# Pacing the FFN matmuls between the counting steps of a balanced router, its third token list in one go, and idle matmuls ahead of the first transposes

## The chip, the cores and the metric

One core of one Trainium2 chip. The metric is device microseconds of one execution, the median of several runs. A profile is one execution, so its span differs a little from the median. Several chips were used; each experiment is compared with runs of the kernel before on the same chip. Where two experiments ran on different chips, only their ratios to that kernel are compared, and what chips differ by is in no interval.

Words used below. An idle matmul is one whose result nobody reads. Half clock, or cold, means a granted clock of TensorE of 0.50; the cold stretches behind 200 us last 3.4 us or two to four times that, and one such unit is called a window.

## The reference, cut to what matters

An attention block makes `x` (3072 tokens of 384). A router then gives each of 8 experts exactly 384 tokens, in the order of the scores, and each expert runs its FFN on its tokens.

```python
logits = x @ w_gate
order = np.argsort(-logits.flatten())
for idx in order:                       # greedy, with a capacity of N // E per expert
    tok, e = idx // E, idx % E
    if assigned[tok] >= 0 or counts[e] >= cap: continue
    assigned[tok] = e; counts[e] += 1
for e in range(E):
    h = np.maximum(x[assigned == e] @ w1[e], 0.0)
    out[assigned == e] = h @ w2[e]
```

## The kernel before

The attention part (to about 165 us) is not touched. The router runs in seven rounds and a rest. A round makes `choices`, searches a threshold in two searches of four steps, assigns tokens, and closes one expert, whose token list is then built, so that the rows of `x` can be gathered and its FFN can run. The FFN is a queue of 51 pieces (3 transposes, 24 up, 24 down); TensorE runs pieces of it between the steps. A step finds one digit of the threshold, and ends with a matmul that hands this digit to VectorE. An assignment begins with matmuls into `sums`; a list ends with matmuls into `tokens`, behind which three gathers (DMAs that fetch 128 rows of `x` each) are issued. The order on TensorE and VectorE is the order of the program.

```python
def counts_beside(r, above, choice, slots):
    ...                                   # 3 matmuls, L501: lhsT = above, rhs = choice
    some(dve_work, 1)
    tt(own, ...); reduce(part, ...)       # VectorE
    some(pe_work, slots)
    nc.tensor.matmul(out=cnt, lhsT=pick_th, rhs=part, ...)               # L513

def search(choice, over, slots):
    for shift, slots in zip((12, 8, 4, 0), slots):
        tt(above, over, steps[shift], ALU.is_ge)                         # VectorE
        if slots:
            some(pe_work, slots[0])
            cnt = counts_beside(r, above, choice, slots[1])
        else:
            cnt = counts_alone(r, above, choice)
        some(dve_work, 1)
        tt(fills, ...); reduce(filled, ...)                              # VectorE
        if slots:
            some(pe_work, slots[2])
        nc.tensor.matmul(out=digit, lhsT=units[shift], rhs=filled, ...)  # L535
        some(dve_work, 1)
        tt(new, over, digit, ALU.add)                                    # VectorE
        over = new
    return over

# expert_list(): [members, place, index, lines] + six times in_line + [used, tokens]
#   place:  a matmul (L600);  index: starts the DMA of the expert's weights
#   tokens: 24 small matmuls (L653), three gathers by GpSimd, pe_work.extend(ffn(L))
# ffn(L):   [turn(0..2)] + [up(ft, d)] * 24 + [down(i, ft)] * 24

def idle_turns(n):
    for _ in range(n):
        nc.tensor.matmul(out=bank("idle", "H")[:, 0:CAP], lhsT=ones[:],
                         rhs=idle[:, 0:CAP], start=True, stop=True)
...
slots = (2, 1, 1)
for rnd in range(E - 1):
    ...                                   # choices, keys: VectorE
    over = search(choice, high, [slots if rnd else None] * 4)
    stt(over[:], over[:], 65536.0, low[:], ALU.mult, ALU.add)
    over = search(choice, over, [slots if rnd else None] * 4)
    some(dve_work, len(dve_work))
    assign(choice, over, (1, 8))          # starts with the matmuls into sums (L549)
    dve_work.extend(expert_list())
    if rnd == 0:
        while dve_work:
            some(dve_work, 1)
            idle_turns(3)
        idle_turns(12)
        ...
    if rnd == 1:                          # "in one go": the list is built at once
        while dve_work:
            some(dve_work, 1)
            some(pe_work, 1)
    close()                               # otherwise it is built in the next round's steps
```

Of the kernel before, what the change touches and what calls it, by code (L numbers as in the profile page):

```python
# [23 lines left out]
def kernel(  # L24
# [29 lines left out]
    nc = tc.nc  # L54

    B, H, S, DH = q.shape
# [10 lines left out]
    CAP = N // E  # L67
    TE = CAP // 128
# [14 lines left out]
    def const(shape, dtype, name):  # L83
        return consts.tile(shape, dtype, name=name, tag=name)
# [223 lines left out]
    ones = const([128, 128], BF16, "ones")  # L308
# [49 lines left out]
    idle = const([128, CAP], BF16, "idle")  # L358
# [5 lines left out]
    def col(t, *shape):  # L364

        return t.rearrange("p (c o) -> p c o", o=1).to_broadcast((128, NT) + shape)

    def row(t, n):

        return t.rearrange("p (o n) -> p o n", o=1).to_broadcast((128, NT, n))  # L370
# [5 lines left out]
    def rt(shape, name, dtype=FP32, bufs=2):  # L376
        return route.tile([128] + shape, dtype, name=name, tag=name, bufs=bufs)
# [4 lines left out]
    def tt(out_, a, b, op):  # L382
        nc.vector.tensor_tensor(out=out_, in0=a, in1=b, op=op)  # L383
# [8 lines left out]
    def reduce(out_, in_, op):  # L392
        nc.vector.tensor_reduce(out=out_, in_=in_, axis=AX_X, op=op)
# [11 lines left out]
    def high_keys(best, key, half, high):  # L405

        bits = best.bitcast(I32)
        ts(key, bits, 31, ALU.arith_shift_right, -2147483648, ALU.bitwise_or)
        tt(key, bits, key, ALU.bitwise_xor)
        ts(half, key, 16, ALU.logical_shift_right)  # L410
        nc.vector.tensor_copy(out=high, in_=half)
# [40 lines left out]
    def assign_and_run(begun, also=None, again=None):  # L452
# [5 lines left out]
        def bank(name, tag):  # L458
            return psum.tile([128, 512], FP32, name=name, tag=tag, bufs=BUFS[tag])
# [5 lines left out]
        pe_work, dve_work = deque(), deque()  # L465

        def some(queue, n):
            for _ in range(min(n, len(queue))):
                queue.popleft()()

        def choices():

            masked = rt([NT, E], "masked")
            tt(masked[:], logits[:], row(penalty[:], E), ALU.add)
            best = rt([NT], "best")
            reduce(best[:], masked[:], ALU.max)
            tt(masked[:], masked[:], col(best[:], E), ALU.is_equal)
            tt(masked[:], masked[:], row(first[:], E), ALU.mult)
            pick = rt([NT], "pick")
            reduce(pick[:], masked[:], ALU.max)  # L480

            taken = rt([NT], "taken")
            reduce(taken[:], assigned[:], ALU.max)
            stt(pick[:], taken[:], 100.0, pick[:], ALU.mult, ALU.add)
            choice = rt([NT, E], "choice", BF16)
            tt(choice[:], masked[:], col(pick[:], E), ALU.is_equal)
            return choice, best

        def counts_alone(r, above, choice):

            cnt = r[0:NTH, 0:E]
            for c in range(NT):
                nc.tensor.matmul(out=cnt, lhsT=above[:, c, :], rhs=choice[:, c, :],
                                 start=(c == 0), stop=(c == NT - 1))
            return cnt

        def counts_beside(r, above, choice, slots):

            m, n = NTH * CG, E * CG
            for c in range(0, NT, CG):  # L500
                nc.tensor.matmul(out=r[0:m, 0:n],  # L501
                                 lhsT=above[:, c:c + CG].rearrange("p c n -> p (c n)"),
                                 rhs=choice[:, c:c + CG].rearrange("p c e -> p (c e)"),
                                 start=(c == 0), stop=(c == NT - CG))
            some(dve_work, 1)
            own = rt([CG, E], "own")
            tt(own[0:m], r[0:m, 0:n].rearrange("p (g e) -> p g e", e=E), mine8[0:m], ALU.mult)
            part = rt([E], "part", FP16)
            with nc.allow_low_precision("a single count"):
                reduce(part[0:m, :], own[0:m].rearrange("p g e -> p e g"), ALU.max)  # L510
            some(pe_work, slots)
            cnt = r[0:NTH, n:n + E]
            nc.tensor.matmul(out=cnt, lhsT=pick_th[0:m, :], rhs=part[0:m, :], start=True, stop=True)  # L513
            return cnt

        def search(choice, over, slots):

            for shift, slots in zip((12, 8, 4, 0), slots):
                above = rt([NT, NTH], "above", BF16)
                tt(above[:], col(over[:], NTH), row(steps[shift][:], NTH), ALU.is_ge)  # L520
                r = bank("cnt", "r")
# [6 lines that stand above are left out]
                fills = rt([E], "fills")  # L528
                tt(fills[0:NTH, :], cnt, wanted[0:NTH, :], ALU.is_ge)
                filled = rt([1], "filled", BF16)  # L530
                reduce(filled[0:NTH, :], fills[0:NTH, :], ALU.max)
                if slots:
                    some(pe_work, slots[2])
                digit = r[:, 128:129]
                nc.tensor.matmul(out=digit, lhsT=units[shift][0:NTH, :],  # L535
                                 rhs=filled[0:NTH, :], start=True, stop=True)
                some(dve_work, 1)
                new = rt([NT], "over")
                tt(new[:], over[:], digit.to_broadcast((128, NT)), ALU.add)
                over = new  # L540
            return over
# [182 lines left out]
                   mybir.EngineType.Pool}  # L724
        def idle_turns(n):

            for _ in range(n):
                nc.tensor.matmul(out=bank("idle", "H")[:, 0:CAP], lhsT=ones[:],  # L728
                                 rhs=idle[:, 0:CAP], start=True, stop=True)

        with tc.manual_schedule(engines=engines):
            if begun is None:
                begun, part = begin()
                part(0, NCH)
            slots = (2, 1, 1)
            for rnd in range(E - 1):
                if rnd == 0:
                    choice, key, high = begun
                else:
                    choice, best = choices()  # L740
                    key, half, high = rt([NT], "key", I32), rt([NT], "half", I32), rt([NT], "high")
                    high_keys(best[:], key[:], half[:], high[:])
                low = rt([NT], "low")
                low_keys(key[:], low[:])
                over = search(choice, high, [slots if rnd else None] * 4)

                stt(over[:], over[:], 65536.0, low[:], ALU.mult, ALU.add)
                over = search(choice, over, [slots if rnd else None] * 4)
                some(dve_work, len(dve_work))
                assign(choice, over, (1, 8))  # L750
                dve_work.extend(expert_list())
                if rnd == 0:
                    while dve_work:
                        some(dve_work, 1)
                        idle_turns(3)
                    idle_turns(12)
                    if also:
                        dve_work.append(lambda: also(bank("hits", "r")))
                if rnd == 1:
                    while dve_work:  # L760
                        some(dve_work, 1)
                        some(pe_work, 1)
                close()
# [5 lines that stand above are left out]
            choice, _ = choices()  # L769
            tt(assigned[:], assigned[:], choice[:], ALU.add)  # L770
            nc.vector.memset(full[:], 1.0)
            some(pe_work, 4)
# [4 lines that stand above are left out]
            if again is not None:  # L777
                again.append(nc.values_load(beyond[0:1, 0:1], min_val=0, max_val=128))
            some(pe_work, len(pe_work))
# [18 lines left out]

    again = []
    assign_and_run(begun, in_range, again)  # L800


# [61 lines left out]
    with tc.If(again[0] > 0):  # L864
# [7 lines left out]
        with tc.For_i(0, B, 1) as b:  # L872
            x = pool.tile([128, NCH, D], FP32, name="xb", tag="xb", bufs=1)
            with tc.For_i(0, HP, 1) as hp:
                scan_pair(pool, x, b, hp)
            nc.sync.dma_start(
                out=xd[:, :].rearrange("(b c t) d -> b t c d", b=B, c=NCH)[
                    bass.ds(b, 1)].rearrange("b t c d -> (b t) c d"),
# [35 lines left out]
```

## Time and profile before

| | before |
|---|---|
| median, range of 4 runs | 568.57 us, 568.34 to 569.75 |
| span of the profiled run | 566.8 us |
| mean granted clock of TensorE | 0.938 |
| TensorE busy | 495.4 us, 87% |

The prediction shows the main lines. One view more, the waits (who waited, for what: us in total, times, longest), has the two waits that this case is about:

```profile
PE Xe L686 <- DMA xe<-xd,token: 13.8, 9, 4.9
...
PE cnt L501 <- DVE above L383: 3.5, 5, 1.1
```

The first is TensorE with an empty queue, waiting for gathered rows. The second is a count waiting for VectorE.

### The profile page before, as it was taken

The numbers are of one execution on the slowest core, as the hardware profiler recorded it, in microseconds if no ns is written. First come the engines' busy times: TensorE is split into PE (matmuls) and PEld (weight loads), VectorE is DVE, ScalarE is ACT, GpSimd is POOL, SyncE is SP. The second block draws the span as 40 slices with busy tenths as digits, with TensorE's granted clock in tenths as the row PEclk, the third lists the DMA queues.
The fourth block names the chain that finished last, engine by engine and source line by source line (L and its number), as shares of the span: only waits on it lengthen the run. The fifth ranks groups of instructions, "written<-read, shape, count | busy, mean of one in ns | idle before, by whom it ended". The sixth has DMA issues, their size and how long they took to land.

```text
span 566.8 us, 12225 instructions
## 1 busy us (share of the span) xinstructions
PE 495.4 (87%) x5031; PEld 310.8 (55%) x5031; DVE 290.5 (51%) x990; ACT 128.2 (23%) x301; POOL 114.2 (20%) x172
## 2 busy tenths in 40 slices
PE   3999999999974669969995798989989989999993
PEld 2688788888863334444542444545445556555551
DVE  6666566566754744572477267477585682000000
ACT  3455455543410011101200110111021021120310
POOL 3243333422300020050012101302212142101001
PEclk9999999999985579996999698999999999999998
DMA  8888998751010340070006106206134187100000
GB/s 176 178 184 173 206 194 173 166 126 50 32 45 1 114 151 0 1 279 26 1 14 250 43 0 235 73 1 236 56 127 153 37 279 258 42 0 29 14 15 31
DMA packets 118352, 59.08 MB, mean 104 GB/s; under 512 B 101648, under 2 KB 112912, under 8 KB 118288
## 3 DMA queue, kind: packets, MB, share of 16 engines
q1 hardware_dynamic: 111760, 44.06, 29.4%
q0 software_dynamic: 3072, 9.44, 5.1%
q10 hardware_dynamic: 3456, 4.72, 2.3%
q8 instruction: 41, 0.67, 0.5%
q14 instruction: 23, 0.19, 0.1%
HBM read 48.77 MB, written 9.44 MB: 103 GB/s over the span
## 4 chain that ended last, share of the span: by engine, by line
PE 61%; issue 18%; DVE 13%; POOL 4%; DMA 2%; ACT 1%; POOLq 0%; DVEq 0%; ACTq 0%
PE H L697 15%; PE O L708 13%; PE Y L239 4%; PE T L185 4%; PE A L222 3%; PE L L153 3%; PE Y L249 2%; PE L L157 2%; PE X L265 2%; PE dS L204 2%; DMA xe<-xd,token 2%; POOL out_dram L713 2%; PE idle L728 2%; POOL xe L663 1%; PE X L279 1%
## 5 line engine op out<-in xcount | busy, mean ns | idle before, releaser
L697 PE MATMUL H<-xeT,w 128*128 128x384 f32 x384 | 151.4, 526 | 4.9 <-ACT xeT L689 4.9
L708 PE MATMUL O<-w,hT 128*128 128x384 f32 x384 | 141.5, 506 | 0.0
L697 PEld LDWEIGHTS H<-xeT,w 128*128 128x128 f32 x384 | 69.1, 197 | 40.2 <-ACT xeT L689 6.4
L708 PEld LDWEIGHTS O<-w,hT 128*128 128x128 f32 x384 | 68.7, 192 | 37.0 <-issue 2.8
L713 POOL DMA_INDIRECT out_dram<-o,token x24 | 25.4, 1058 | 192.6 <-ACT o L712 192.0
L701 ACT ACTIVATE hT<-H 128x384 f32<-128x384 f32 x64 | 31.4, 491 | 135.9 <-PE H L697 134.4
L227 DVE COPY_PREDICATED am<-mask,A 128x512 f32<-128x512 int32 x48 | 32.4, 728 | 31.3 <-PE A L222 31.3
L712 ACT COPY o<-O 128x384 f32<-128x384 f32 x24 | 11.5, 479 | 141.7 <-PE O L708 141.7
L663 POOL DMA_INDIRECT xe<-xd,token x24 | 24.0, 1002 | 47.1 <-DVE over L383 26.0
L383 DVE TENSOR_TENSOR in_line<-line,count 128x512 bf16<-128x512 f32 x48 | 32.0, 699 | 0.1
L177 POOL TENSOR_TENSOR kg<-k,ek 128x384 f32<-128x384 f32 x24 | 25.5, 1065 | 27.2 <-ACT ek L165 21.4
L383 DVE TENSOR_TENSOR own<-cnt,mine 120x64 f32<-120x64 f32 x48 | 10.7, 222 | 38.9 <-PE cnt L501 38.7
L153 PE MATMUL L<-g,wcum 128*128 128x384 f32 x48 | 22.5, 551 | 7.9 <-DVE count L322 7.9
L501 PEld LDWEIGHTS <-above 128*120 128x120 bf16 x144 | 15.7, 142 | 22.1 <-DVE above L383 9.6
L239 PE MATMUL Y<-v,am 128*64 128x48 f32 x768 | 27.7, 224 | 0.0
L383 DVE TENSOR_TENSOR above<-over,steps 128x360 bf16<-128x360 f32 x49 | 26.1, 533 | 1.7
L239 PEld LDWEIGHTS Y<-v,am 128*64 128x64 f32 x768 | 24.5, 138 | 4.1 <-issue 3.7
L222 PE MATMUL A<-qT,kT 48*64 48x128 f32 x768 | 25.8, 272 | 0.0
L686 PE MATMUL Xe<-ident,xe 128*128 128x128 f32 x72 | 13.5, 324 | 13.8 <-DMA xe<-xd,token 13.8
L689 ACT COPY xeT<-Xe 128x384 f32<-128x384 f32 x24 | 10.8, 488 | 62.5 <-PE Xe L686 62.3
L162 DVE TENSOR_SCALAR dl<-L 128x384 f32<-128x384 f32 x24 | 13.4, 557 | 19.4 <-PE L L157 19.4
L629 POOL TENSOR_TENSOR past<-b,ramp_nt 128x48 f32<-128x48 f32 x8 | 2.4, 305 | 101.1 <-DVE b L383 83.6
(164 smaller groups left out, 633.4 us busy)
## 6 DMA issues: line engine op xcount, KB each, us to landing
w<-in_moe_w_dram SPq DMA_DIRECT2D x16, 1536.0 KB, 6.9
f<-in_f_logit_dram SPq DMA_DIRECT2D x24, 192.0 KB, 3.8
q<-in_q_dram SPq DMA_DIRECT2D x24, 192.0 KB, 3.9
k<-in_k_dram SPq DMA_DIRECT2D x24, 192.0 KB, 4.1
v<-in_v_dram SPq DMA_DIRECT2D x24, 192.0 KB, 4.0
xd<-x ACTq DMA_DIRECT2D x24, 192.0 KB, 3.4
xe<-xd,token POOLq DMA_INDIRECT x24
out_dram<-o,token POOLq DMA_INDIRECT x24
```

The costliest lines, as they stand in the source:

```text
L153: nc.tensor.matmul(out=Lv, lhsT=wcum[:], rhs=g[:, :, 0:DH], start=True, stop=True)
L177: nc.gpsimd.tensor_tensor(out=kg[:, :, 0:DH], in0=G["k"][:], in1=ek[:], op=ALU.mult)
L185: nc.tensor.transpose(out=T[:, 128 * hp:128 * hp + 128], in_=t[:, 2 * hp:2 * hp + 2, :].rearrange("t h d -> t (h d)"), identity=ident[:])
L222: nc.tensor.matmul(out=A[par][HC * j:HC * j + HC, 128 * hp:128 * hp + 128], lhsT=G["kT"][rows, hp, HC * j:HC * j + HC], rhs=G["qT"][rows, ...
L227: nc.vector.copy_predicated(am[:, par], mask[:].unsqueeze(1).to_broadcast((128, HP, 128)), A[par][:].rearrange("s (a t) -> s a t", t=128))
L239: nc.tensor.matmul(out=Y[par][HC * j:HC * j + HC, DH * hp:DH * hp + DH], lhsT=G["am"][:, par, hp, HC * j:HC * j + HC], rhs=G["v"][:, 2 * h ...
L383: nc.vector.tensor_tensor(out=out_, in0=a, in1=b, op=op)
L663: nc.gpsimd.indirect_dma_start(out=xe[:], out_offset=None, in_=xd[:, :], in_offset=bass.IndirectOffsetOnAxis(ap=token[:, i:i + 1], axis=0))
L697: nc.tensor.matmul(out=L["H"][:, 0:CAP], lhsT=L["w1"][:, d, 128 * ft:128 * ft + 128], rhs=xT[:, d, :], start=(d == 0), stop=(d == DC - 1))
L701: nc.scalar.activation(out=hT[:, ft, :], in_=L["H"][:, 0:CAP], func=AF.Relu)
L708: nc.tensor.matmul(out=L["O"][:, 0:D], lhsT=hT[:, ft, 128 * i:128 * i + 128], rhs=L["w2"][:, ft, :], start=(ft == 0), stop=(ft == FC - 1))
L713: nc.gpsimd.indirect_dma_start(out=outs[next(tiles)][:, :], out_offset=bass.IndirectOffsetOnAxis(ap=L["token"][:, i:i + 1], axis=0), in_=o ...
```

## The change

The intent: spend fewer pieces between the steps of rounds two and three, so that some are left when the next gather is under way; build the third list at once, as the second is; and keep TensorE from idling ahead of the first transposes. (The idle matmuls also write one tile of another pool now.)

```diff
         def idle_turns(n):
+            nothing = bank("nothing", "O")
             for _ in range(n):
-                nc.tensor.matmul(out=bank("idle", "H")[:, 0:CAP], lhsT=ones[:],
-                                 rhs=idle[:, 0:CAP], start=True, stop=True)
+                nc.tensor.matmul(out=nothing[:, 0:CAP], lhsT=ones[:], rhs=idle[:], start=True,
+                                 stop=True)
...
-            slots = (2, 1, 1)
+            pace = {0: None, 1: (1, 1, 1), 2: (1, 1, 1)}
...
-                over = search(choice, high, [slots if rnd else None] * 4)
+                slots = [pace.get(rnd, (2, 1, 1))] * 4
+                over = search(choice, high, slots)
...
-                over = search(choice, over, [slots if rnd else None] * 4)
+                over = search(choice, over, slots)
...
-                    idle_turns(12)
+                    idle_turns(27)
+                    for _ in range(TE - 1):
+                        some(pe_work, 1)
+                        idle_turns(4)
...
-                if rnd == 1:
+                if rnd in (1, 2):
```

## The prediction

> **What bounds the kernel now.** I read first the page of the run: the slices of busy tenths and clock, and the chain that ended last.
>
> ```profile
> PE   3999999999974669969995798989989989999993
> PEclk9999999999985579996999698999999999999998
> ...
> PE 61%; issue 18%; DVE 13%; POOL 4%; DMA 2%; ACT 1%; POOLq 0%; DVEq 0%; ACTq 0%
> ```
>
> A slice is 14.2 us. TensorE is full in the attention part (to about 165 us) and again from about 320 us on. Between lie dips in both rows. The first (slices 12 and 13) is the counting of the first round, which has no FFN work beside it yet; the change leaves it alone. The dips near 205, 255 and 310 us are what it aims at. Busy time by stretches of 10 us sizes two of them (columns: length, PE, PEld, DVE, ACT, POOL busy with counts, granted clock, DMA share, GB/s):
>
> ```profile
> 250.00:260.00 10.00, 4.20 (x34) 2.95 (x31) 4.84 (x21) 1.89 (x4) 3.94 (x4) 0.73 0.62 213
> 310.00:320.00 10.00, 5.27 (x23) 3.14 (x20) 2.16 (x11) 1.44 (x3) 2.90 (x3) 0.50 0.22 62
> ```
>
> Then the timeline of TensorE, at these three places (start, duration, line, tile, count, idle time before it and who ended it). The first is from a stretch at 184 us, the other two from one at 235 us:
>
> ```profile
> 199.44 2.60 PE L728 MATMUL idle<-idle,ones 128*128 128x384 bf16 x15
> 204.40 0.52 PE L686 MATMUL Xe<-ident,xe 128*128 128x128 f32 x3 [2.36 <-DMA xe<-xd,token]
> ...
> 207.40 0.87 PE L686 MATMUL Xe<-ident,xe 128*128 128x128 f32 x3 [0.77 <-DMA xe<-xd,token]
> ```
> ```profile
> 249.77 0.75 PE L653 MATMUL tokens<-number,in_line 128*128 128x6 bf16 x24
> 255.38 0.90 PE L686 MATMUL Xe<-ident,xe 128*128 128x128 f32 x3 [4.87 <-DMA xe<-xd,token]
> ...
> 303.41 0.91 PE L708 MATMUL O<-w,hT 128*128 128x384 f32 x2
> ...
> 309.33 0.81 PE L653 MATMUL tokens<-number,in_line 128*128 128x6 bf16 x24
> 313.90 0.90 PE L686 MATMUL Xe<-ident,xe 128*128 128x128 f32 x3 [3.76 <-DMA xe<-xd,token]
> ```
>
> Each expert's FFN is a queue of 51 pieces: 3 transposes, 24 up, 24 down. A piece (two instructions) costs 15.75/24 = 0.656 us where nothing interrupts. The queue runs dry twice: from 250.5 to 255.4 the second expert's gather is awaited, and from 304.3 to 313.9 hardly anything but counting runs, because the third list is built within the steps. The first idle time, 202.0 to 204.4, awaits the first gather.
>
> Last, what a step of the search costs when fed:
>
> ```profile
> 267.01 0.17 PE L535 MATMUL cnt<-filled,unit 15*128 15x1 bf16 x1
> 267.12 1.56 PE L697 MATMUL H<-xeT,w 128*128 128x384 f32 x4
> 268.51 0.30 PE L501 MATMUL cnt<-choice,above 128*120 128x64 bf16 x3
> 268.65 0.89 PE L697 MATMUL H<-xeT,w 128*128 128x384 f32 x2
> 269.47 0.17 PE L513 MATMUL cnt<-part,pick_th 120*15 120x8 f16 x1
> 269.57 0.91 PE L697 MATMUL H<-xeT,w 128*128 128x384 f32 x2
> 270.42 0.17 PE L535 MATMUL cnt<-filled,unit 15*128 15x1 bf16 x1
> ```
>
> 3.41 us from digit to digit: legs of 1.50 (two pieces), 0.96 and 0.95 (one each). Four pieces are 2.62 us, so 0.79 us is lost per step.
>
> **What the Trainium skill says.** "TensorE: Matmul & The Clock Gate", Part 1: activity is judged in free-running windows of 3413 ns, and a quiet one drops the clock to 4/8. The trace agrees: the granted clock is 0.50 in stretches, read in half microseconds, of about 206.7 to 213.5, 254.5 to 264.7, 309.1 to 322.7 and 343.2 to 346.6 us, that is 2, 3, 4 and 1 windows, on one grid. The same page, Part 4, says transposes do not count as busy in the same way; here the window ending at 206.7, with six of nine transposes in it, did go cold. "DMA: Bandwidth & Descriptors", "Anatomy of one DMA": about 2 us of fixed cost per transfer; that agrees: a gather's issue on GpSimd runs from 310.81 for 0.99 us, and TensorE can use the rows at 313.90, 2.1 us after that.
>
> From the trace I take a rule of thumb: counting each matmul's streaming time, the windows that went cold were up to about 0.35 full (that ending at 343.2 had 0.34), those with 0.39 to 0.46 stayed. This is an estimate.
>
> **The change part by part**, with S1, S2, S3 for the start of the assignment (first matmul into sums) of rounds two to four, which lies at 236.61, 288.28 and 332.14 us before. I counted the queue through both programs: pieces left there are 19, 18 and 35 before, 25, 31 and 29 after.
>
> (a) Idle matmuls. 15 took 2.60 us, so 30 (27 and the 3 of the list) end at 199.44 + 4.9 = 204.3, when the first gather lands: no gap. Four more (0.65 us each time) fit in the waits for the second and third gather (205.85, 207.40). The three landings do not move. But the clock stays high, so the half-clock stretch to 213.5 goes. Third transpose at 207.4, first up piece at 208.5, first digit of round two at 210.15 (210.42 before, with one piece fewer done after).
>
> (b) Steps of three pieces in rounds two and three. The leg with two pieces gets one. It is then bound by VectorE: over starts 0.21 us after the digit, above ends at 267.97, 0.96 after it, so the leg is about 1.03 and the step 0.96 + 0.95 + 1.03 = 2.94. A step loses 2.94 - 1.97 = 0.97, that is 0.18 us more than before; 16 steps cost 2.9 us. S1 is 210.15 + 7 x 2.94 + 0.2 (one more VectorE operation between the searches) + 0.84 = 231.8.
>
> (c) The second list. From sums to tokens took 13.16 us (236.61 to 249.77) with 19 pieces; one more makes 13.8, tokens at 245.6. Now five pieces are left, so the gather no longer is awaited. **But another wait takes its place**: the next count needs choices, keys and above from VectorE, and in round two that took from 198.83 (tokens) to 204.36 (end of above), 5.55 us. Only two pieces cover it: tokens 0.61 + 1.31 = 1.9, idle 3.65 us. Count at 251.2. By the rule of thumb a gap of this size goes cold with a chance of 0.95, for about 3.5 us in which steps lose some 0.43 of the time (a leg of 0.95 us takes 1.69 at half clock, 260.85 to 262.54): 1.5 us. S2 = 251.2 + 7 x 2.94 + 1.91 + 0.2 + 1.5 + 0.84, less 0.3 for the shorter transposes = 275.9.
>
> (d) Third list in one go. Again 13.8, tokens at 289.7, with 11 pieces left; three cover the wait, idle 3.0 us, count at 295.3; cold with 0.7, so 1.1 us. Round four keeps steps of four: S3 = 295.3 + 7 x 3.41 + 1.91 + 1.1 + 0.84 = 323.0. The hole of 304 to 314 us and the half clock to 322.7 go.
>
> Sum at S3: 332.14 - 323.0 = 9.1 earlier, with 6 pieces fewer left (3.9 us): **13.0 us gained**.
>
> (e) Given back in round five. The fourth list comes in the steps, as before, but only 4 pieces are left at its tokens (10 before). Four pieces and the counts last 4.04 us; the gather comes at 4.6, 5.8 and 7.1 us after tokens (as 309.33 to 313.90, 315.12, 316.46). That stalls 2.1 us, and the thin stretch goes cold with about 0.65: 1.0 more. Later lists have 14 and more pieces left.
>
> (f) The start of a round can go cold by the window's phase (it did once before, at 343, for 1.6 us). Expected over three rounds after: 1.3. Net 0.3 gained.
>
> 13.0 - 3.1 + 0.3 = 10.2 us, so 568.6 - 10.2 = **558.4**; I say 558.0.
>
> **The rivals.** (1) The clock stays up in the new gaps: for it, 0.39 stayed up; against it, gaps of 3 us and more nearly fill a window. It is worth 1.5 + 1.1 + 1.0, so about 554.5. (2) VectorE becomes the bound in rounds two and three more than I think (a step of 3.1, or the list slower than its 13.8): each 0.1 us a step costs 1.6, so 560 to 561. The in-line comparisons on VectorE, 6 of 0.66 us after the line, end about 5.3 us after the place matmul, against 6.5 us of pieces: so unlikely for the list. (3) The gathers were hidden anyway, and only the idle matmuls count: 566. Against it, the 4.87 and 3.76 us waits are named for the gather, and TensorE is full at the end, so that saved time is not absorbed.
>
> **Range and chances.** The parts add to 10 us; the clock is worth up to 4 either way, the step 2, the gather 1. I take 554 to 562. The 2% line is 557.2, inside the range and a little below the middle: faster 0.41, within 2% 0.58, slower 0.01.
>
> **What the profile after would show.** No idle time over 0.5 us at 202 to 204.4, and clock 1.0 to 213: (a). Digit to digit 2.94 us in rounds two and three: (b). Waits of 3.0 to 3.7 us on above (VectorE) behind the second and third tokens, in place of waits on the gather: (c), (d). A wait on the gather in the second search of round five, 2 us in all: (e). Half clock after each of these. S3 near 323. The prediction is wrong if the clock does otherwise, or if the steps of three pieces take over 3.1 us or under 2.8.

## The result, and the profile after

| | before | after |
|---|---|---|
| median, range of 4 runs | 568.57 us, 568.34 to 569.75 | 559.01 us, 558.99 to 559.98 |
| span of the profiled run | 566.8 us | 557.1 us |
| mean granted clock | 0.938 | 0.958 |
| idle matmuls behind the first tokens | 15 | 38 |

The ratio is 0.9832, 95% interval 0.9815 to 0.9849. A ratio is the mean time of one kernel's runs over that of the other's of the same rounds, so not quite the ratio of the medians. The change is thus inside 2%, to which the prediction gave 0.58. The page of the run after:

```profile
PE   3999999999993489998997989889899989999993
...
PEclk9999999999995599998999999899989999999997
...
PE 64%; issue 18%; DVE 11%; POOL 4%; DMA 1%; ACT 1%; POOLq 0%; ACTq 0%; DVEq 0%
```

The dips near 205 and 310 us are gone from both rows; shallower ones are left, in the busy row near 255 and 300 us. The stretches by 10 us that the prediction showed of before, and the place in round five that it warned of (columns as there):

```profile
250.00:260.00 10.00, 6.68 (x29) 3.68 (x30) 5.82 (x25) 1.92 (x4) 2.92 (x3) 0.83 0.33 111
310.00:320.00 10.00, 10.00 (x40) 5.00 (x39) 4.53 (x19) 1.96 (x4) 0.00 (x0) 1.00 0.00 1
347.00:357.00 10.00, 7.97 (x31) 3.94 (x30) 3.55 (x14) 1.91 (x4) 3.89 (x4) 0.83 0.26 82
```

From 310 to 320 us TensorE goes from 5.27 busy at clock 0.50 to 10.00 at 1.00. The waits have changed places:

```profile
PE cnt L501 <- DVE above L383: 8.5, 7, 3.6
...
PE Xe L686 <- DMA xe<-xd,token: 3.0, 4, 1.4
```

The wait on gathers falls from 13.8 to 3.0 us, the wait on VectorE rises from 3.5 to 8.5, its longest from 1.1 to 3.6. The timeline of TensorE shows where: at the first gather, behind the second and the third tokens, and at the fourth gather.

```profile
200.32 5.04 PE L729 MATMUL nothing<-idle,ones 128*128 128x384 bf16 x30
206.75 0.55 PE L686 MATMUL Xe<-ident,xe 128*128 128x128 f32 x3 [1.39 <-DMA xe<-xd,token]
...
247.24 0.75 PE L653 MATMUL tokens<-number,in_line 128*128 128x6 bf16 x24
247.85 1.54 PE L708 MATMUL O<-w,hT 128*128 128x384 f32 x4
252.96 0.35 PE L501 MATMUL cnt<-choice,above 128*120 128x64 bf16 x3 [3.58 <-DVE above L383]
```
```profile
291.78 2.18 PE L708 MATMUL O<-w,hT 128*128 128x384 f32 x6
296.90 0.35 PE L501 MATMUL cnt<-choice,above 128*120 128x64 bf16 x3 [2.94 <-DVE above L383]
...
345.54 0.76 PE L653 MATMUL tokens<-number,in_line 128*128 128x6 bf16 x24
...
350.13 0.55 PE L686 MATMUL Xe<-ident,xe 128*128 128x128 f32 x3 [0.38 <-DMA xe<-xd,token]
351.39 0.55 PE L686 MATMUL Xe<-ident,xe 128*128 128x128 f32 x3 [0.71 <-DMA xe<-xd,token]
...
353.67 1.65 PE L697 MATMUL H<-xeT,w 128*128 128x384 f32 x2 [0.47 <-ACT xeT L689]
```

The two waits on above are the predicted ones, 3.58 and 2.94 us long. In the last line a piece takes 1.65 instead of 0.91 us: the clock is at half. A step of three pieces, from digit to digit, takes 217.54 - 214.58 = 2.96 us:

```profile
214.58 0.17 PE L535 MATMUL cnt<-filled,unit 15*128 15x1 bf16 x1
214.68 0.91 PE L697 MATMUL H<-xeT,w 128*128 128x384 f32 x2
215.59 0.35 PE L501 MATMUL cnt<-choice,above 128*120 128x64 bf16 x3
...
217.54 0.17 PE L535 MATMUL cnt<-filled,unit 15*128 15x1 bf16 x1
```

**The ledger.** S0 to S6 are the starts of the seven assignments. The table has the lengths between them, and behind each the pieces run in it.

| us (pieces) | S0 at | S0-S1 | S1-S2 | S2-S3 | S3-S4 | S4-S5 | S5-S6 | S6 to end |
|---|---|---|---|---|---|---|---|---|
| before | 185.93 | 50.68 (32) | 51.67 (52) | 43.86 (34) | 38.67 (41) | 37.04 (41) | 37.05 (41) | 121.93 |
| after | 187.71 | 45.72 (26) | 43.93 (45) | 46.22 (53) | 40.08 (41) | 36.64 (41) | 38.84 (41) | 117.99 |

With a piece at 0.656 us: S0-S1 gains 50.68 - 45.72 - 6 x 0.656 = 1.0 us, S1-S2 gains 7.74 - 7 x 0.656 = 3.1, S2-S3 gains 19 x 0.656 - 2.36 = 10.1. The next three give back 1.4, gain 0.4 and give back 1.8. The rest is 3.94 shorter because 6 pieces (3.94 us) fewer are left. In all 11.5 us; but S0 itself came 1.78 us later in this execution, so the span shows 9.7. The change touches nothing ahead of S0. There the granted clock reached full speed 22.4 us after the start, against 15.7 in the trace before. This is chance: the fourteen traces are of programs that are the same up to S0, and S0 lies between 185.75 and 191.78 us; the earliest had full speed from 15.7 us on, the latest from 31.3.

### The profile page after: what moved, and what is told of

It reads as the page before. It is cut to its first block, busy times and chain, and to the rows that moved or that the text cites. A ratio compares the mean times of both kernels' runs of the same rounds, so it can differ in the third digit from the quotient of the medians.

```text
span 557.1 us, 12270 instructions
## 1 busy us (share of the span) xinstructions
PE 497.1 (89%) x5054; PEld 310.7 (56%) x5054; DVE 292.8 (53%) x990; ACT 128.4 (23%) x301; POOL 114.4 (21%) x172
## 4 chain that ended last, share of the span: by engine, by line
PE 64%; issue 18%; DVE 11%; POOL 4%; DMA 1%; ACT 1%; POOLq 0%; ACTq 0%; DVEq 0%
PE H L697 17%; PE O L708 14%; PE Y L239 4%; PE T L185 4%; PE A L222 3%; PE L L153 3%; PE Y L249 2%; PE L L157 2%; PE X L265 2%; PE dS L204 2%; PE cnt L501 2%; POOL out_dram L713 2%; PE X L279 1%; PE nothing L729 1%; DMA xe<-xd,token 1%
## 5 line engine op out<-in xcount | busy, mean ns | idle before, releaser
L712 ACT COPY o<-O 128x384 f32<-128x384 f32 x24 | 11.5, 478 | 143.3 <-PE O L708 138.0
L501 PEld LDWEIGHTS <-above 128*120 128x120 bf16 x144 | 13.9, 135 | 29.0 <-DVE above L383 20.8
L501 PE MATMUL cnt<-choice,above 128*120 128x64 bf16 x144 | 15.6, 218 | 8.5 <-DVE above L383 8.5
```

Source lines behind the costliest of these rows:

```text
L501: nc.tensor.matmul(out=r[0:m, 0:n], lhsT=above[:, c:c + CG].rearrange("p c n -> p (c n)"), rhs=choice[:, c:c + CG].rearrange("p c e -> p ( ...
```

## The experiments

All outputs are right. Times are medians; "before" was timed on the same chip in the same rounds.

| run | us (range) | ratio to before, 95% interval |
|---|---|---|
| idle part alone | 567.0 (565.8 to 570.9) | 0.9954 (0.9913 to 0.9996) |
| pace alone | 556.9 (555.3 to 558.0) | 0.9767 (0.9733 to 0.9800) |
| list in one go alone | 578.3 (577.1 to 579.5) | 1.0147 (1.0112 to 1.0181) |
| idle and pace, no list in one go | 558.0 (552.6 to 559.5) | 0.9767 (0.9723 to 0.9812) |
| pace and list, no idle part | 560.9 (558.6 to 561.7) | 0.9841 (0.9807 to 0.9876) |
| the whole change, again | 562.8 (560.8 to 565.9) | 0.9874 (0.9837 to 0.9911) |
| whole, idle matmuls in the new waits | 558.8 (554.2 to 560.4) | 0.9794 (0.9753 to 0.9835) |
| whole, shorter steps ahead of the fourth list | 560.0 (558.0 to 564.8) | 0.9849 (0.9808 to 0.9891) |
| whole, four pieces of each list deferred | 553.9 (550.3 to 558.4) | 0.9719 (0.9668 to 0.9770) |
| idle, pace, second list deferred | 551.6 (550.5 to 556.8) | 0.9678 (0.9645 to 0.9712) |
| the same, shorter steps in round six | 555.9 (554.0 to 556.8) | 0.9753 (0.9720 to 0.9786) |
| the same (not shorter steps), idle by the fifth transposes | 550.5 (549.7 to 553.0) | 0.9661 (0.9625 to 0.9696) |

The first four were on one chip; again, idle in the waits, and the two deferred ones on a second; shorter steps (both) and no idle part on a third; the last on a fourth.

My theory: TensorE sets the end, and the gain is stall time taken from it, place by place, by how many pieces are left where a gather or VectorE is awaited. Rival one: the clock is what matters, and the idle matmuls carry the gain. Rival two: the third list in one go is what fills the hole at 304 to 314 us.

### The parts one at a time

**The idle part alone:** `pace = {0: None}` and `if rnd == 1:` in the changed kernel.

> The kernel before with the idle part alone (27 idle matmuls, first two transposes brought forward with 4 idle matmuls each); four pieces a step and the third list in the steps stay. My theory: only the half clock of 206.7 to 213.5 us goes, about 2 us; the queue still runs dry at both places, so 566 to 567 us. Rival (the clock is what the change is about, the idle matmuls carry it): 560 to 562.

Measured: 567.0 us. The queue still runs dry; the gather behind the second tokens is awaited, with the clock dropping as before:

```profile
249.87 0.26 PE L653 MATMUL tokens<-number,in_line 128*128 128x6 bf16 x4 [0.21 <-DVE in_line L383]
255.76 2.18 PE L686 MATMUL Xe<-ident,xe 128*128 128x128 f32 x9 [5.63 <-DMA xe<-xd,token]
```

Rival one is out as the cause of the gain: alone, the idle part is worth half a per cent.

**The pace alone:**

```diff
-            slots = (2, 1, 1)
+            pace = {0: None, 1: (1, 1, 1), 2: (1, 1, 1)}
...             # and the two calls of search with pace.get(rnd, (2, 1, 1)); idle matmuls as before
```

> The kernel before with three pieces a step in rounds two and three alone. My theory: 27 pieces are left at the assignment of round two, 7 at the second tokens, 24 at the start of round four, 8 at the third tokens, so the queue never runs dry and no gather is awaited, although the third list is built in the steps: about 556 us, that is faster than the whole change (559.0). Rival (the third list in one go is what fills the hole at 304 to 314 us, the pace only feeds it): 564 to 567.

Measured: 556.9 us, ratio 0.9767, with an interval that lies below both of the whole change (0.9815 to 0.9849, and 0.9837 to 0.9911 in the second measurement). By these ratios, taken on different chips, the pace alone is worth more than the three parts together. The traces show only that it is worth as much: from S0 to the end they have 368.9 us here, and 369.4 and 374.3 in the two of the whole change. The third list is built in the steps here, and TensorE goes on behind its tokens:

```profile
300.30 0.76 PE L653 MATMUL tokens<-number,in_line 128*128 128x6 bf16 x24
300.92 1.54 PE L708 MATMUL O<-w,hT 128*128 128x384 f32 x4
302.39 0.35 PE L501 MATMUL cnt<-choice,above 128*120 128x64 bf16 x3
```

**The list in one go alone:** `if rnd in (1, 2):` in the kernel before.

> The kernel before with the third list in one go alone. My theory: with four pieces a step only 9 pieces are left when the list begins, the queue runs dry in the list and the third gather is awaited as the second was, and round five has the hole that round four had: slower, 575 to 578 us. Rival (the list in one go fills the hole): 558 to 562.

Measured: 578.3 us, slower by 1.5%. Behind the third tokens TensorE has nothing left and waits for the gather:

```profile
302.08 0.75 PE L653 MATMUL tokens<-number,in_line 128*128 128x6 bf16 x24
308.13 1.58 PE L686 MATMUL Xe<-ident,xe 128*128 128x128 f32 x6 [5.30 <-DMA xe<-xd,token]
```

The hole of round four is not filled but moved: S3-S4 is 43.91 us here, as S2-S3 was before (43.86). With the run before, where the hole is gone without this part, rival two is out.

**The whole without the list in one go:** `if rnd == 1:` in the changed kernel.

> The changed kernel without its third list in one go (built in the steps of round four again). My theory: 22 pieces at the start of round four are enough; the 3 us wait for above behind the third tokens goes (1.3 us net), and with 16 instead of 4 pieces at the fourth tokens the wait for the fourth gather and its half clock go (3 us): about 554.7 us, 553 to 557. Rival (the list in one go is needed): 566 or more.

Measured: ratio 0.9767, so 0.65 points below the whole change's first result and 1.1 below its second; the median of 558.0 us is above the 553 to 557 that I gave, on a chip where before itself took 570.1. S2-S3 and S3-S4 are 37.23 and 37.06 us: no wait behind the third tokens and none at the fourth gather, as expected. In the profiled run (559.0 us) it was the clock that lay outside: S1-S2 took 47.90 us, because 13.7 us of it were at half clock.

**The whole without the idle part:** `idle_turns(12)` and no transposes ahead.

> The changed kernel without its idle part (12 idle matmuls as before, no transposes brought forward); pace and third list in one go stay. Theory: round two is 1.9 us worse (half clock at 207 us back), but 6 pieces instead of 4 are left at the fourth tokens, which takes 2 us of waiting and some half clock away: within 2 us of the changed kernel, ratio to before 0.981 to 0.988. Rival (parts add up): 3 us slower than the changed kernel, as the idle part alone gained 0.5%.

Measured: 0.9841, the same as the whole (0.9832 and 0.9874). S0-S1 is 46.48 us, 0.8 longer than after (45.72) and, with 24 pieces run in it instead of 26, two pieces behind, in all 0.8 + 2 x 0.656 = 2.1 us; S3-S4 is 37.11 instead of 40.08 us: with 6 pieces left at the fourth tokens its gather is not awaited. So the idle part's gain is given back through the queue, within what these intervals resolve. The parts do not add up.

### The clock

**The whole change, again**, unedited:

> The changed kernel as it is, again, to have its time and its clock stretches on the chip of the other runs. Theory (which windows go cold depends on where their grid falls, and that differs from run to run): the stretches at half clock lie elsewhere or are of other length than in the first trace, runs spread over 3 us or more, ratio 0.980 to 0.986. Rival (the stretches belong to the program): the same three stretches after 206 us, spread under 1.5 us.

Measured: 560.8 to 565.9 us, ratio 0.9874, a little worse than I gave. The granted clock, read in windows of half a microsecond, was at half behind 206 us (the tail after the last matmul left out) in these stretches: first trace 254.5 for 3.4, 353.5 for 3.4, 401.3 for 6.8 us; this trace 252.7 for 6.8, 300.5 for 3.4, 338.0 for 3.4, 358.5 for 6.8, 409.7 for 3.4 us. The same program, 13.7 us in one and 23.9 in the other. S1-S2 is the same sequence of instructions in four profiled runs, and only the clock differs:

| run | half clock in S1-S2 | S1-S2 |
|---|---|---|
| after | 3.4 us | 43.93 us |
| shorter steps ahead of the fourth list | 3.4 | 44.27 |
| the whole change, again | 6.8 | 45.21 |
| idle and pace | 13.7 | 47.90 |

The wait behind the second tokens is 3.58 us in each. A look at the last one, with its slow pieces:

```profile
252.04 0.51 PE L501 MATMUL cnt<-choice,above 128*120 128x64 bf16 x3 [3.58 <-DVE above L383]
252.36 1.63 PE L708 MATMUL O<-w,hT 128*128 128x384 f32 x2
...
260.77 1.65 PE L697 MATMUL H<-xeT,w 128*128 128x384 f32 x2
```

**Idle matmuls in the new waits**, behind each of the two lists of the changed kernel:

```diff
+                    gap = bank("gap", "H")
+                    for _ in range({1: 20, 2: 16}[rnd]):
+                        nc.tensor.matmul(out=gap[:, 0:CAP], lhsT=ones[:], rhs=idle[:], start=True,
+                                         stop=True)
```

> The changed kernel with idle matmuls (20 and 16, 3.2 and 2.6 us) laid into the two new waits behind the second and third tokens. Theory: the waits stay as long (0.3 us left of each in the trace), but no window goes cold there: 1.5 to 3 us faster than the changed kernel of the same rounds. Rival (the wait itself is all that costs, half clock is hidden by VectorE): same within 0.5 us.

Measured: ratio 0.9794, against 0.9874 for the whole change of the same rounds, so 0.8 points, 4 us at the medians, more than I gave; the intervals are apart by little (0.9835 and 0.9837), and part of it is round five (S3-S4), where the second trace of the whole change had 10.2 us of half clock and this one none. The wait itself stays: from tokens to the count are 5.72 us in both, 247.24 to 252.96 and 250.45 to 256.17. S1-S2 falls to 42.95 us, and in the profiled run there is no half clock between 201 and 402 us.

```profile
251.78 3.41 PE L772 MATMUL gap<-idle,ones 128*128 128x384 bf16 x20
255.03 0.81 PE L708 MATMUL O<-w,hT 128*128 128x384 f32 x2
256.17 0.35 PE L501 MATMUL cnt<-choice,above 128*120 128x64 bf16 x3 [0.33 <-DVE above L383]
```

So half clock costs (47.90 - 42.95) / 13.7 = 0.36 us per us in steps of three pieces (0.29 to 0.39 by the other three traces of the table).

### The waits that took the place of the old ones

**Four pieces of each list deferred** behind its tokens, so that VectorE gets there sooner and TensorE has work while it makes the next above:

```diff
-                assign(choice, over, (1, 8))
+                assign(choice, over, (1, 7 if rnd in (1, 2) else 8))
...
                 if rnd in (1, 2):
-                    while dve_work:
-                        some(dve_work, 1)
-                        some(pe_work, 1)
+                    for n in range(len(dve_work)):
+                        some(dve_work, 1)
+                        some(pe_work, 1 if n > 2 else 0)
+                    some(pe_work, 4)
```

> The changed kernel with four FFN pieces of each list of rounds two and three moved from ahead of the tokens to behind them (same pieces in all). Theory: sums to tokens falls from 13.8 to about 11.6 us, VectorE then being the bound of the list, and the wait for above behind tokens falls from 3.6 and 2.9 to about 1.0 and 0.4 us: 2.2 us a list and less half clock, 4 to 7 us faster than the changed kernel, 552 to 555. Rival (the list takes 13 us of VectorE anyway): no gain.

Measured: 553.9 us, ratio 0.9719 against 0.9874 of the same rounds. S1-S2 falls from 43.93 to 40.49 us with the same 45 pieces, S2-S3 from 46.22 to 44.65. The waits are 1.00 us, as expected, and 1.24 where I gave 0.4.

**The same for the second list, and the third in the steps again** (`rnd == 1` in both places).

> Both findings together: third list in the steps again, four pieces of the second list moved behind its tokens. Theory: 2.2 us and the half clock after the second tokens off the kernel of idle matmuls and pace alone (ratio 0.977 to before), and 6 us or more off the changed kernel: ratio to before 0.967 to 0.972, 550 to 554 us. Rival (the list in one go is worth keeping): slower than the kernel with deferred pieces alone.

Measured: 551.6 us, ratio 0.9678, of the same rounds as the run before; their intervals overlap (0.9719, from 0.9668), so the two are not told apart in time. In the traces S2 to S4 is 74.45 us with 82 pieces, against 84.90 with 94: 2.6 us less than the 12 pieces account for. From sums (237.59) to tokens is 11.35 us, and the wait is the 1.0 us expected:

```profile
248.94 0.75 PE L653 MATMUL tokens<-number,in_line 128*128 128x6 bf16 x24
249.54 4.12 PE L708 MATMUL O<-w,hT 128*128 128x384 f32 x12
254.66 0.35 PE L501 MATMUL cnt<-choice,above 128*120 128x64 bf16 x3 [1.00 <-DVE above L383]
```

**Shorter steps ahead of the fourth list**, in the changed kernel:

```diff
-                over = search(choice, high, slots)
+                over = search(choice, high, [(1, 1, 1)] * 4 if rnd == 4 else slots)
```

> The changed kernel with three pieces a step in the first search of round five as well, so that 8 pieces instead of 4 are left at the fourth tokens. Theory (the fourth gather is awaited because the queue is too short there): the wait on the gather (2 us) and the half clock behind it go, four steps cost 0.18 us each: 2 to 5 us faster than the changed kernel, ratio to before 0.977 to 0.983 (the changed kernel had 0.983 and 0.987). Rival (the wait is the DMA's own slowness at that place): slower by 0.7 us.

Measured: ratio 0.9849, between the two results of the whole change (0.9832, 0.9874), outside what I gave. The time is inconclusive. The mechanism shows in the trace: no transposes of the fourth expert wait for the gather, and S3-S4 is 38.41 us with 4 pieces fewer, of which 6.8 us were at half clock, which fell at the start of that round this time.

### What was left: transposes at a thin place

The two traces with the idle part, the pace and the third list in the steps had S5-S6 at 40.0 us. (The pace alone had 36.73: there these transposes begin at 401.59 us, behind the first count of round seven, and no window went cold.) The fifth expert's transposes, 0.49 us each against 0.656 for other pieces, stand where round seven starts and TensorE waits for VectorE; 6.8 us were at half clock behind them. In the kernel with the deferred second list:

```profile
396.48 0.49 PE L686 MATMUL Xe<-ident,xe 128*128 128x128 f32 x3
397.91 0.35 PE L501 MATMUL cnt<-choice,above 128*120 128x64 bf16 x3 [0.94 <-DVE above L383]
...
399.66 0.17 PE L513 MATMUL cnt<-part,pick_th 120*15 120x8 f16 x1 [1.04 <-DVE part L393]
```

**Move them**, by shorter steps in the first search of round six (`[(1, 1, 1)] * 4 if rnd == 5 else slots`):

> Third list in the steps, four pieces deferred behind the second tokens, and three pieces a step in the first search of round six, so that the transposes of the fifth expert no longer stand at the thin start of round seven, where a window went cold in both traces with the third list in the steps (40.0 us between assignments, against 36.7 to 37.1 of its neighbours). Theory: that interval falls to 37, four steps cost 0.7 us: 1.5 to 3 us faster than with deferred pieces and list in the steps alone; 548 to 551, ratio 0.962 to 0.967. Rival (the half clock only moves to another place): same as that kernel, 0.968.

A miss: 555.9 us, ratio 0.9753. S5-S6 fell only to 38.37, still with a cold window of 3.4 us. The longer queue put the next expert's transposes into the last list, where TensorE waited for VectorE and the clock dropped again for 6.8 us:

```profile
439.52 0.82 PE L686 MATMUL Xe<-ident,xe 128*128 128x128 f32 x6
442.47 0.18 PE L600 MATMUL before<-total,ltri 128*128 128x1 bf16 x1 [2.13 <-DVE e L387]
```

The rival of that run was right that the half clock moves; its number (0.968) was not. S6 to the end took 131.86 us with 177 pieces, against 125.62 with 173 in the kernel without shorter steps: 3.6 us more than four pieces cost.

**Fill them**: the kernel with the deferred second list, with idle matmuls behind these transposes.

```diff
+                    if L["place"] == 4:           # at the end of turn(i)
+                        idle_turns((5, 5, 2)[i])
```

> Third list in the steps and four pieces deferred behind the second tokens, with 12 idle matmuls (5, 5 and 2) laid behind the three transposes of the fifth expert, into the waits of 0.9, 1.0 and 0.5 us at the start of round seven. Theory: the window that was 0.20 full there stays warm, the interval from the sixth to the seventh assignment falls from 40.0 to about 37.3 us at the same order of work: 2 to 3 us faster, ratio to before 0.961 to 0.966. Rival (as with the longer queue: the half clock comes back at another place): 0.968 and over, with a new cold stretch after 430 us.

Measured: 550.5 us, S5-S6 37.24, no half clock between 200 and 543 us. (The window that I called 0.20 full was 0.25 full by the estimate of the last section.) The ratio of 0.9661 is just above what I gave, and its interval overlaps that of the kernel without the fill (0.9678), so the gain in time is not settled; the interval between the assignments is. This is the fastest version by its median.

```profile
393.42 0.98 PE L731 MATMUL nothing<-idle,ones 128*128 128x384 bf16 x5
394.52 0.35 PE L501 MATMUL cnt<-choice,above 128*120 128x64 bf16 x3
```

## Why the prediction was right, point by point

The prediction was 558.0 us in a range of 554 to 562; the result was 559.01. The second measurement, 562.8 us on another chip, is 0.8 us outside the range; before took 569.9 there, and not 568.6.

- **(a)** The clock stayed up, as said. The gather did not land on time, against the first of the signs that the prediction named: TensorE was idle for 1.39 us, as the first rows could be used 4.86 us after their issue (201.89 to 206.75), against 3.39 before. The other two transposes then followed without a wait, so S0-S1 is 45.72 us, against 231.8 - 185.93 = 45.9.
- **(b)** 2.94 us a step was predicted; 2.97 was measured in nearly every step, and 3.19 between the searches (predicted 3.14).
- **(c)** Sums to tokens 13.80 us (predicted 13.8), the new wait 3.58 (3.65), S1-S2 43.93 (275.9 - 231.8 = 44.1). That VectorE sets the wait that takes the place of the removed one is confirmed in two ways: filled with idle matmuls, the count comes no sooner and no later (5.72 us behind tokens); with four pieces moved across tokens, it shrinks to 1.00 us.
- **(d)** The wait was 2.94 us (3.0). The half clock that I priced at 1.1 us did not come in the first trace (S2-S3 46.22, predicted 47.1), and came in the second (47.82, 3.4 us of half clock): an even-handed estimate, whose size per run is 0 or 1.6.
- **(e)** Confirmed: waits on the fourth gather at 350.1 to 352.6 us, 1.56 us in all (2.1 predicted), and half clock behind them. S3-S4 was 40.08 and 43.22 us in the two traces, against 37.11 in the run with 6 pieces left at those tokens. So 3.0 and 6.1 us, where I gave 3.1; the first trace had 3.4 us of half clock there, the second 10.2.
- **(f)** The clock in later rounds: I expected 0.3 us of net gain; the first trace lost 1.8 us in S5-S6. I had put this down to the start of a round; the half clock there begins at 401.3 us, just where the fifth expert's transposes (398.1 to 401.3 us) now stand. Where transposes come to lie was missing from my list.
- **Not foreseen:** S0 differs between executions, by up to 6.0 us in the fourteen traces; that the clock in the attention part makes this fits the two ends given above, and is not tested. It hid part of the gain in the profiled pair: 11.5 us between S0 and the end, where I said 10.2, and 9.7 in the span.
- **Luck in the total:** up to S3 the first trace gained 14.3 us (unrounded) where I said 13.0, mostly because the half clock of (d) did not come. From S3 on it gave back 2.8, as I had summed, but out of other terms: 1.4 lost, 0.4 gained, 1.8 lost, where I had 3.1 lost and 0.3 gained. The later S0 took another 1.8. That 558.0 is so near 559.01 owes something to these cancelling.
- **A page read too easily:** I let the window ending at 206.7 us stand as agreeing that transposes do not count as busy in the same way. By the estimate of the last section it was 0.22 full even with its transposes counted, so it tests nothing. Other windows do, and speak against it (see there).

The rivals of the prediction: the clock in the gaps did stay up in some executions, so (1) is half true, run by run. (2) and (3) did not happen.

What I did not ask in the prediction, and the runs answer: whether each part was needed. The third list in one go, once the pace is there, brings nothing, and by the ratios (0.9767 without it, 0.9832 and 0.9874 with it, on different chips) costs time; with it comes the 2.94 us wait, and the queue that is too short at the fourth tokens.

## What to carry to other kernels

Count the filler work that is left at each place where the busy engine can be made to wait; a filler spent early at a place that needs little is missing later at one that needs much, and a part that helps alone (or hurts alone) can do the opposite beside another. When a wait is taken away, look for the one that ended just before it: here VectorE's chain behind the tokens took the gather's place, and moving four pieces across it in two lists (from 0.9874 to 0.9719, in the same rounds) was worth about as much as the change. Short pieces (transposes) in a thin stretch can let the clock drop; either fill there or look where else they would land before moving them.

## What the Trainium skill lacked or had wrong

- "TensorE: Matmul & The Clock Gate", its table of why this matters, advises to avoid idle gaps of over about 3 us. Here much shorter gaps let the clock drop: in the trace before the clock went to 0.50 at 343.3 us, where the longest gap of TensorE ahead of it was 0.67 us; what counted was how full the window was as a whole. This is an estimate from the traces: a matmul is counted with its columns at 5.04 / 30 = 0.168 us for 384, as in the idle matmuls, and a 32-bit one with twice that (a piece is two of them, 0.656 us). Then, behind 200 us in all fourteen traces, each window ahead of a drop was at most 0.39 full (that of 397.9 to 401.3 us in the trace after was), and each that was 0.40 full or more stayed; of those below only one, at 0.38, stayed.
- The same page, Part 4, says that full speed does not engage for transposes, which do not count as busy in the same way. Here, where they run as 32-bit matmuls against an identity, they count: with the second list deferred, the window of 352.1 to 355.5 us held nine transposes and little else, 0.43 full with them and 0.13 without, and the clock stayed at 1.00; the window of 334.6 to 338.0 us in the second trace of the whole change, 0.39 full without any transpose, was followed by half clock.
- The same page, "Terms", prices throttled time at 1 - K/N, so 0.5 us per us at half clock. Here it is 0.36 in steps of three pieces, where, as I read it, VectorE sets a part of the pace.
- The same page, Part 1, has a variation from run to run for the warm-up at a kernel's start. None has it for the stretches in the middle of a tuned kernel: the same program had 13.7 and 23.9 us of half clock behind 206 us in two executions, and one kernel's runs on one chip ranged from 552.6 to 559.5 us.
- "DMA: Bandwidth & Descriptors", "Anatomy of one DMA", gives a fixed cost of about 2 us for a transfer. The first gather, issued 7.4 to 8.9 us after the 3 MB of the expert's weights, could be used 3.4 to 5.2 us after its issue (3.1 where no such load was near), and always 11.8 to 12.8 us after the issue of the weights, in all 14 traces. That the gather stands behind the weights fits this; no run here tests it.
